# Relu²-attention and an MLP mixer on one core: another written order of all engines, with 56 stretches of small tiles

## The chip, the core and the metric

The kernel runs on one core of one Trainium2 chip. The metric is the device time of one execution in microseconds. A core has engines that run side by side, each with its own instruction stream: PE (TensorE, the matrix unit), DVE (VectorE), ACT (ScalarE), POOL (GpSimd, here only for issuing loads) and SP (SyncE, here for issuing transposes and stores). Matmuls write into PSUM, eight banks of 128 partitions by 512 fp32 columns; ACT and DVE read PSUM and write the on-chip memory SBUF, from which PE reads. An engine works through its stream in order. Where an instruction needs something another engine or a DMA has not finished, it waits, and all that is behind it on that engine waits too.

## The reference

Attention without softmax (relu, squared) over 8 batches, 12 heads, 448 positions and heads of 64, then a mixer over tokens and over channels:

```
scores = (q @ k.T) / sqrt(64)
attn   = maximum(scores, 0) ** 2 / 448
x      = (attn @ v)  -> (8, 448, 768)          # heads side by side
xt     = x.transpose(0, 2, 1)
h      = maximum(xt @ w_tok1, 0) @ w_tok2      # 448 -> 256 -> 448
u      = x + h.transpose(0, 2, 1)
out    = u + maximum(u @ w_ch1, 0) @ w_ch2     # 768 -> 1536 -> 768
```

Inputs and output are fp32; the kernel computes in bf16 with fp32 accumulation in PSUM.

## The kernel before

**Steps.** The attention is cut into 24 steps s of four heads, three to a batch. Each of its operations has a name with the step and a number behind it. The order in which all engines get their work is a string, `ORDER` (lines 73 to 242), with one word for each operation; `Order.run` (line 50) goes through the words and emits each operation's instructions, so the string is the order in every engine's stream at once. `:A` and `:D` send an operation to ACT or DVE; digits name the PSUM banks that it writes; a load's `:name` makes it wait until the SP operation of that name has been issued and done (line 971). Nothing moves the words at run time: what the planner of the string decided, the engines do. Dependencies, and the waits for a buffer's or a bank's former users, are semaphores.

The words, in the order in which a step goes through them:

- `ldk`, `ldq`, `ldv` (POOL, line 371): loads of half a step's k, q or v, 112 KB each, cast to bf16 on the way; four buffers for each. `ldf`, `cast` (ACT, DVE): step 0's q comes by SP as fp32 and is cast (lines 349 and 351 are the copies on ACT and on DVE that `cast`, `cp`, `xc`, `ik` and `iq` share). `wt1`, `wt2`, `wc1`, `wc2`: weights, `wc` in thirds of 768 KB.
- `T` (PE, line 472) and `cp`: steps 0 to 9 transpose k and q on PE, and `cp` copies them out of PSUM. From step 10 on `ik`, `iq` (a copy on ACT or DVE) and `xk`, `xq` (a transposing DMA issued by SP, line 497) do this. Three buffers (`NQ`) hold the transposed k and q, so `xk`, `xq` of step s wait for the last score of step s - 3.
- `S` (PE, line 515): scores, seven a step, four matmuls of 64 by 64 on quarters of the array, into two banks. `r` (two to an S): relu out of PSUM, on ACT (line 343) or DVE (345). `q` followed by two numbers: the square, on ACT (355) or DVE (357).
- `V` (PE, line 542): attention times v, again on quarters of the array, seven a step, accumulated in two banks. `xe`: eviction with the scale (ACT 552, DVE 554).
- `X` and `xc` (steps 0 to 5: PE transposes and copies them) or `xd` (from step 6: a transposing DMA of SP, line 566): x with the tokens on the partitions.
- `t1` (PE, 588), `rt` (relu on ACT), `t2` (PE, 597), `u` (DVE, 601): token mixing and the residual. `ub` (SP, line 610): u transposed back by DMA, for the last add.
- `C1`, `c1e` (line 623): channel mixing, first matrix, for batches 0 and 1. `M1`, with `tu`, `s1`, `d1`, `y1`, `w1` (function `fast1`, products at line 780): the same for batches 2 to 7 with seven products instead of eight; `tu` and `w1` are sums made ahead, `s1`, `d1`, `y1` take the products out of PSUM.
- `M2`, with `d2`, `h`, `w2` (function `fast2`, products at line 847; `d2` are DVE adds, lines 860 and 862) and, for tiles that have no partner, `C2`, `c2e`: channel mixing, second matrix, likewise, and the last add of u. `st` (SP, line 668): stores from four output buffers.
- `fill:bank*count` (line 967): matmuls on a buffer of zeros into a free bank, whose result nobody reads; a count of 4 is 512 columns, the rest units of 128.

**Stretches.** S, V and T work on small tiles (64 by 64 on a quartered array), all other products of PE on the full array. A stretch is a run of S, V and T with none of the others between them.

**What follows from the order.** SP's queue holds `xk`, `xq`, `xd`, `ub` and `st` in the order of the words; POOL's holds the loads. The operations of step s + 1 and later are written between those of step s, so that the evictions of one fill the time of PE's products of the other. The first 40 us have only attention and token mixing; the products of the channels begin when batch 0's u is there (`C1.0.3` is the first before).

The two places that the change touches in the code:

```python
    def run(self, fill):
        done = set()
        for word in ORDER.split():
            name, _, how = word.partition(':')
            if name == 'fill':
                bank, _, count = how.partition('*')
                fill(int(bank), int(count))
                continue
            o = self.ops[name]
```

```python
        for n in [512] * (count // 4) + [128] * (count % 4):
            nc.tensor.matmul(ps[:, :n], lhsT=warm[:, :128], rhs=warm[:, :n], start=True, stop=True)
```

Of the kernel before, what the change touches and what calls it, by code (L numbers as in the profile page):

```python
# [123 lines left out]
q9.6:D c1e1.11:A u6.1:D c1e1.8:A t2.7.0:1 ub1.4 c1e1.7:D V9.0:05 V9.1 u7.0:D S10.1:27 V9.2 V9.3 r10.1.1:A
h0.3.0:D S10.5:46 st2.64 V9.4 r10.1.0:A V9.5 r10.5.0:D V9.6 st0.0 S11.0:31 S10.4:72 xe9.1:A xe9.0:D M2.0.3.2:4
xk12 r10.4.1:A r10.5.1:D r11.0.1:A r11.0.0:D t2.7.1:5 r10.4.0:A d2.0.3.11a:D S10.0:02 xd9 S10.6:61 h0.3.1:D
S10.3:37 r10.0.0:A M2.0.3.5:4 u7.1:D r10.0.1:A ldk14.1:ub1.4 q11.0:A r10.6.0:D xq12 M2.0.3.1:0 ldv10.1:st2.64
iq13:D r10.3.1:A ik13:D r10.3.0:A M2.0.5.2:2 ub2.0 d2.0.3.11b:D r10.6.1:A h0.5.0:D S11.1:56 h0.3.2:D S10.2:73
t1.8.0:1 r10.2.1:A xk13 h0.3.3:D r11.1.0:A r10.2.0:D M2.0.3.6 rt8.0:A d2.0.5.11a:D ub2.2 r11.1.1:A q10.0:D
t2.8.0:3 q10.4:A d2.0.3.12a:D M2.0.5.1:5 d2.0.3.22a:D ub2.1 ldv11.1:xq12 u8.0:D S11.2:71 t2.8.1:2 ldq14.0  # L130
r11.2.0:A M2.0.3.3 r11.2.1:A u8.1:D ldv10.0:xq12 xq13 q10.2:A h0.5.1:D ldq14.1 t1.9.0:6 d2.0.5.11b:D q10.1:A
ldv11.0:xq12 tu2.2:D S11.3:37 ldk16.1:xk13 ik14:D S11.4:12 r11.3.1:A M2.0.3.7 h0.5.2:D ldv12.1:ub2.2 q11.2:A
r11.4.0:D ldq16.1:xk13 M2.0.5.6 r11.4.1:A d2.0.3.22b:D ldk16.0:ub2.1 r11.3.0:A h0.5.3:D M2.0.5.5:7 rt9.0:A
d2.0.5.12a:D q10.3:A ldq15.1 M2.0.3.4 d2.0.5.22a:D q11.4:A q11.1:D ldk15.1 M2.0.5.3 d2.0.3.12b:D q10.6:A
tu2.0:D ldv12.0:ub2.2 S12.0:12 d2.0.3.21:D q10.5:A V10.0:36 V10.1 w1.2.2:D V10.2 ldq15.0 S11.5:40 M2.0.5.7
r11.5.0:A r11.5.1:D ldq17.0:ub2.1 r12.0.0:A d2.0.5.12b:D ldk17.0 iq14:A M1.2.0.5:4 d2.0.5.22b:D ldk15.0
w1.2.1:D V10.3 r12.0.1:A V10.4 S11.6:01 q11.3:D V10.5 V10.6 xq14 S12.2:72 w1.2.0:D xe10.1:A M2.0.5.4 xe10.0:D
r12.2.0:A r11.6.1:D xk14 M1.2.0.1:6 s1.2.0.5:A tu2.1:D M1.2.2.1:3 r12.2.1:D s1.2.0.1:A M1.2.0.2:7 r11.6.0:D
# [865 lines left out]
```

## Time and profile before

| what | value |
| --- | --- |
| median of 3 runs | 346.09 us (344.8 to 348.53) |
| the profiled execution | span 345.2 us, one core |
| PE | first warm-up product (line 414) starts at 1.19 us, last product ends at 340.98 |
| DMA | 50.19 MB moved in 98939 packets, mean 145 GB/s |
| queue 1 (SP's and the transposes) | 45.8% of 16 engines' span |
| queue 0 (POOL's loads) | 45.2% of 16 engines' span |

The page gives, for each engine, its busy time and share of the span, then the same in 40 slices of 8.6 us, then the chain of work that ended last. PE's busy time counts the fills, and counts a matmul at half clock as busy for twice as long. The view by windows gives for a stretch of time the busy time of PE, PE's weight loads, DVE, ACT and POOL, each with the number of instructions, then the granted clock (1.00 is full), the DMA share and GB/s. A line of the timeline is: start, length, engine, line, operation, output and inputs, number of instructions, and in brackets the idle time before it and what ended that. A line of the chain is: start, length, engine, output or line, number.

### The profile page before, as it was taken

Reading aid. Unit: us, or ns where it says so; the run is one execution under the profiler, and the core shown is the slowest. Engines: PE = TensorE matmul, PEld = TensorE weight load, DVE = VectorE, ACT = ScalarE, POOL = GpSimd, SP = SyncE. Lnnn points to the kernel's source line nnn. Section 1 sums busy time; section 2 is a strip of 40 time slices with the busy share of each in tenths; the row PEclk is TensorE's granted clock in tenths of the full one; section 3 lists DMA queues with packets and bytes.
Section 4 is the critical chain, followed back from the end, with each engine's and each line's share of the span. In section 5 each row is a group of like instructions: output and inputs, shape, how many; then the busy total and the mean of one; then the engine's idle time right before and its main releaser. Section 6 shows DMA issues by size and latency. Waiting matters only on the chain.

```text
span 345.2 us, 9402 instructions
## 1 busy us (share of the span) xinstructions
PE 336.0 (97%) x3794; PEld 218.8 (63%) x3795; DVE 299.9 (87%) x578; ACT 243.4 (71%) x457; POOL 92.1 (27%) x157
## 2 busy tenths in 40 slices
PE   7899999999999999999999999999999999999995
...
GB/s 150 184 187 168 171 175 207 113 168 122 186 196 172 144 174 139 222 190 162 180 200 182 191 87 178 181 138 194 80 99 140 9 88 33 41 121 38 106 160 141
DMA packets 98939, 50.19 MB, mean 145 GB/s; under 512 B 71568, under 2 KB 95952, under 8 KB 98896
## 3 DMA queue, kind: packets, MB, share of 16 engines
q1 hardware_dynamic: 72880, 27.15, 45.8%
q0 software_dynamic: 25136, 21.47, 45.2%
...
q14 instruction: 14, 0.11, 0.1%
...
## 4 chain that ended last, share of the span: by engine, by line
PE 87%; DMA 6%; DVE 4%; SPq 1%; issue 0%; ACT 0%; DVEq 0%
PE m_ps L780 22%; PE m_ps L847 20%; PE sc_ps L515 10%; PE acc_ps L542 10%; PE m_ps L623 8%; PE t_ps L588 6%; PE h_ps L597 5%; PE m_ps L713 5%; DMA out_dram<-out_sb 2%; DMA u_sb<-uT 2%; DMA arena<-in_q_dram 1%; DVE arena L357 1%; PE kqT_ps L472 1%; DVE arena L345 1%; DVE arena L351 1%; PE x_ps L579 1%
## 5 line engine op out<-in xcount | busy, mean ns | idle before, releaser
L343 ACT ACTIVATE arena<-sc_ps 128x448 bf16<-128x448 f32 x238 | 117.3, 569 | 15.5 <-PE sc_ps L515 14.4
L345 DVE TENSOR_SCALAR arena<-sc_ps 128x448 bf16<-128x448 f32 x98 | 59.2, 618 | 4.2 <-PE sc_ps L515 2.6
L357 DVE TENSOR_TENSOR arena<-arena 128x896 bf16<-128x896 bf16 x105 | 61.9, 618 | 0.8 <-ACT arena L343 0.7
L355 ACT ACTIVATE arena<-arena 128x896 bf16<-128x896 bf16 x63 | 58.5, 960 | 0.2
L515 PE MATMUL sc_ps<-arena 64*64 64x448 bf16 x672 | 55.5, 370 | 1.1 <-DVE out_sb L860 0.4
L371 POOL DMA_DIRECT2D arena<-in_v_dram x48 | 29.5, 621 | 95.0 <-DMA out_dram<-out_sb 33.8
L542 PE MATMUL acc_ps<-arena 64*64 64x448 bf16 x672 | 46.2, 357 | 1.3 <-DVE arena L357 1.3
L780 PEld LDWEIGHTS <-wc 128*128 128x128 bf16 x432 | 40.8, 98 | 6.1 <-issue 3.2
L371 POOL DMA_DIRECT2D arena<-in_q_dram x46 | 28.3, 626 | 43.5 <-DMA u_sb<-uT 8.2
L371 POOL DMA_DIRECT2D arena<-in_k_dram x48 | 29.7, 626 | 26.9 <-DMA out_dram<-out_sb 16.1
L515 PEld LDWEIGHTS <-arena 64*64 64x64 bf16 x672 | 20.5, 107 | 21.5 <-issue 14.6
L780 PEld LDWEIGHTS <-ws 128*128 128x128 bf16 x324 | 30.5, 98 | 4.5 <-issue 2.5
L601 DVE TENSOR_TENSOR uT<-h_ps,xT 128x448 bf16<-128x448 f32 x48 | 29.2, 618 | 2.2 <-PE h_ps L597 2.1
L847 PE MATMUL m_ps<-wc,r 128*128 128x384 bf16 x162 | 30.3, 327 | 0.0
L847 PEld LDWEIGHTS <-r 128*128 128x128 bf16 x216 | 20.2, 98 | 15.9 <-issue 3.9
L623 PE MATMUL m_ps<-uT,wc 128*128 128x448 bf16 x144 | 30.1, 353 | 0.0
L542 PEld LDWEIGHTS <-arena 64*64 64x64 bf16 x672 | 20.5, 107 | 15.0 <-issue 6.0
L793 ACT ACTIVATE arena<-m_ps 128x448 f32<-128x448 f32 x18 | 9.4, 546 | 24.7 <-PE m_ps L780 7.6
L597 PE MATMUL h_ps<-wt,r_sb 128*128 128x448 bf16 x96 | 25.4, 353 | 0.0
L588 PE MATMUL t_ps<-x_sb,wt 128*128 128x256 bf16 (+1 forms) x216 | 25.4, 261 | 0.0
L780 PE MATMUL m_ps<-uT,wc 128*128 128x224 bf16 x216 | 25.0, 259 | 0.0
L847 PEld LDWEIGHTS <-sums 128*128 128x128 bf16 x180 | 17.2, 98 | 11.7 <-issue 1.1
...
## 6 DMA issues: line engine op xcount, KB each, us to landing
...
arena<-in_k_dram POOLq DMA_DIRECT2D x48, 112.0 KB, 4.4
arena<-in_v_dram POOLq DMA_DIRECT2D x48, 112.0 KB, 4.4
arena<-in_q_dram POOLq DMA_DIRECT2D x46, 112.0 KB, 4.5
wc<-in_moe_w_ch_dram POOLq DMA_DIRECT2D x6, 768.0 KB, 17.3
...
```

The source lines that it names most:

```text
L343: nc.scalar.activation(out, ps, AF.Relu)
L345: nc.vector.tensor_scalar(out=out, in0=ps, scalar1=0.0, scalar2=None, op0=ALU.max)
L355: nc.scalar.activation(x, x, AF.Square)
L357: nc.vector.tensor_tensor(out=x, in0=x, in1=x, op=ALU.mult)
L371: o.ins = nc.gpsimd.dma_start(out=raws[t][s % NR][64 * half:64 * (half + 1)], in_=src[b, h0:h0 + 2].rearrange('e (p c) d -> p e (c d)', c=KC))
L515: nc.tensor.matmul(o.ps[e][64 * half:64 * (half + 1), :S], lhsT=lhsT, rhs=rhs, start=True, stop=True, skip_group_check=True)
L542: nc.tensor.matmul(o.ps[half][64 * e:64 * (e + 1), :S], lhsT=r[rows, e, c * D:(c + 1) * D], rhs=sq[rows, e, :], start=c == 0, stop=c == KC ...
L588: nc.tensor.matmul(o.ps[:, j, :], lhsT=wt1[:, c, j * 128:(j + 1) * 128], rhs=x_sb[:, p0:p1, c, :], start=c == 0, stop=c == 3)
L597: nc.tensor.matmul(o.ps[:, :S], lhsT=r1[:, j, a * 128:(a + 1) * 128], rhs=wt2[:, j, :], start=j == 0, stop=j == JC - 1)
L623: nc.tensor.matmul(ps[:, :S], lhsT=wc1[:, g, e * 128:(e + 1) * 128], rhs=uT[:, g, off:off + S], start=g == 0, stop=g == CC - 1)
L780: nc.tensor.matmul(o.ps[:, j * HB:(j + 1) * HB], lhsT=lhs[:, g, (e + j) * 128:(e + j + 1) * 128], rhs=rhs[:, g], start=j == g == 0 and not ...
L847: nc.tensor.matmul(o.ps[:, :HN], lhsT=lhs[:, e], rhs=rhs[:, e], start=e == 0 and not on, stop=e == EC // 2 - 1, skip_group_check=True)
```

## The change

Only the string `ORDER` is replaced. Both strings hold the same operations; the words stand in another order, many operations change between ACT and DVE, banks are dealt out anew, the gates of the loads name other transposes and stores, and the fills differ. The string is one line longer, so the lines behind it have numbers larger by one.

Counted in the two strings:

| | before | after |
| --- | --- | --- |
| stretches of S, V and T | 68 | 56 |
| of these ahead of `t2.2.1` | 11 | 11 |
| fill words, and units of 128 columns | 4, 16 | 7, 68 |
| `r` on ACT, on DVE | 238, 98 | 216, 120 |
| `q` (square) on ACT, on DVE | 63, 105 | 82, 86 |
| `ik` on ACT | 1 | 7 |
| `c1e` on ACT | 18 | 15 |
| `xe` on ACT | 29 | 32 |
| `y1` on ACT | 11 | 13 |
| `rt` on ACT | 20 | 19 |

The start of both strings, and of the rest of the new one the rounds of `xq18`, `xq19` and `xq20`:

```diff
@@ -71,174 +71,175 @@
 ORDER = """
-ldf.0 ident ldf.1 ldk0.0 ldk0.1 ldk1.0 ldv2.0 cast0.0:D cast0.1:A ldq1.0 ldk1.1 cast1.0:D cast1.1:A ldq1.1
-fill:1*4 T0.0:0 ldv0.1 T0.1:1 cp0.0k:A cp0.0q:D ldv0.0 cp0.1k:D ldq2.0 cp0.1q:D ldk2.0 fill:4*7 S0.3:23
-S0.1:45 S0.6:67 r0.3.0:A r0.3.1:D ldq2.1 S0.5:01 r0.1.0:A r0.1.1:D S0.0:23 wt1.1 r0.6.0:A r0.6.1:D r0.0.0:A
-ldv1.1 q0.1:D r0.0.1:A ldk2.1 q0.3:D r0.5.0:A T1.0:45 r0.5.1:A q0.0:D S0.4:67 ldq3.0 S0.2:23 cp1.0:A cp1.1:D
-ldk3.0 q0.5:D V0.0:01 r0.2.0:A S1.2:54 V0.1 q0.6:D r0.2.1:A ldv1.0 r0.4.0:A r0.4.1:D S1.3:23 ldv2.1 r1.2.0:A
-q0.2:D r1.2.1:A wt1.0 q0.4:D r1.3.0:A V0.2 S1.1:67 ldv3.0 V0.3 q1.2:D r1.3.1:A V0.4 S1.4:54 r1.1.0:A ldk4.1
-r1.1.1:D S1.0:23 r1.4.0:A r1.4.1:D ldk3.1 S1.6:67 r1.0.0:A V0.5 V0.6 q1.1:D r1.0.1:A ldk4.0 xe0.1:D xe0.0:A
-ldq3.1 r1.6.0:A T2.0:54 q1.0:D r1.6.1:A q1.3:D X0.0:2 wt2 X0.1:3 cp2.0:A cp2.1:D S1.5:01 V1.0:67 ldq5.0 V1.1
-q1.4:D r1.5.0:A V1.2 S2.3:45 ldq4.1 V1.3 r1.5.1:A xc0.0:D V1.4 xc0.1:D r2.3.0:A ldk5.1 S2.0:02 q1.5:D r2.3.1:A
-S2.2:13 ldv4.0 q1.6:D r2.0.0:A fill:4*3 V1.5 S2.1:45 r2.0.1:A r2.2.0:D ldq6.1 r2.1.0:A r2.1.1:D S2.6:02 V1.6
-ldv3.1 r2.2.1:A t1.0.0:1 q2.0:D xe1.0:A ldq5.1 S2.4:45 xe1.1:D r2.6.0:A V2.0:36 r2.6.1:A q2.1:D X1.1:0 ldq4.0
-rt0.0:A q2.2:D r2.4.0:A fill:7*2 V2.1 S2.5:72 ldk6.0 q2.3:D r2.4.1:A V2.2 T3.0:14 r2.5.0:A xc1.1:D ldv5.0 V2.3
-q2.4:D r2.5.1:A t2.0.0:5 cp3.0:A ldk5.0 cp3.1:D t1.1.1:0 X1.0:7 u0.0:D wc1.0 rt1.1:A V2.4 S3.2:24 xc1.0:A
-q2.5:D t2.1.1:1 r3.2.0:A q2.6:D ldq6.0 S3.1:50 r3.2.1:A u1.1:D S3.4:72 ldk6.1 V2.5 r3.1.0:A V2.6 q3.2:D ub0.3
-t1.1.0:4 r3.1.1:A ldv4.1 xe2.1:D xe2.0:A S3.0:15 wc1.2 t1.0.1:0 r3.4.0:A r3.4.1:D X2.1:6 rt1.0:A q3.1:D X2.0:3
-r3.0.0:A wc2.0 S3.3:72 xc2.1:D rt0.1:A r3.0.1:A T4.0:41 xc2.0:D wc1.1 q3.4:D r3.3.0:A S3.6:60 t2.0.1:3
-r3.3.1:A cp4.0:D t1.2.1:5 wc2.2 r3.6.0:A u0.1:D S3.5:72 r3.6.1:A cp4.1:D t1.2.0:4 rt2.1:A t2.1.0:6 r3.5.0:A
-q3.0:D t2.2.1:3 rt2.0:A q3.3:D r3.5.1:A S4.1:05 S4.4:17 u1.0:D r4.1.0:A V3.0:42 V3.1 u2.1:D r4.1.1:A ub0.2
...
+fill:3*18 ident ldf.0 ldf.1 cast1.0:D ldk0.0 ldk0.1 cast0.0:D cast1.1:D cast0.1:A T0.0:0 cp0.0k:A T0.1:1
+cp0.0q:A fill:7*7 ldq1.0 ldv0.1 cp0.1k:D cp0.1q:D S0.3:24 r0.3.1:D r0.3.0:A S0.5:56 r0.5.0:D S0.2:30 r0.2.1:D
+r0.2.0:A ldq1.1 q0.3:D ldk2.1 ldk1.0 ldk1.1 S0.1:71 r0.1.1:A ldq2.0 S0.4:24 r0.4.0:A r0.4.1:D fill:3*3 S0.0:50
+r0.0.1:D r0.5.1:A S0.6:13 r0.6.0:A r0.1.0:A T1.0:26 cp1.0:A fill:4*24 cp1.1:D q0.2:D r0.0.0:D S1.1:10 q0.4:A
+q0.1:D r0.6.1:D r1.1.1:A S1.3:76 r1.3.1:A S1.0:24 r1.0.1:A r1.0.0:A r1.1.0:A q0.0:D S1.5:50 ldv0.0 V0.0:63
+r1.5.1:A q0.6:A wt2 ldk2.0 r1.3.0:D ldq2.1 wt1.1 S1.4:42 V0.1 q0.5:D T2.0:71 r1.5.0:D V0.2 V0.3 V0.4 r1.4.0:A
+S1.2:05 V0.5 V0.6 cp2.1:D q1.5:D r1.2.1:A xe0.0:A S1.6:14 r1.2.0:A ldv1.0 q1.1:D ldv2.0 ldv2.1 cp2.0:D S2.1:56
+r1.4.1:D xe0.1:A q1.3:A r2.1.0:D wt1.0 S2.2:07 ldq3.0 ldk3.0 r2.2.0:A r1.6.0:A r1.6.1:A X0.0:3 fill:5*8
+S2.0:25 r2.0.1:A q1.0:D q1.4:D r2.0.0:A r2.2.1:D X0.1:0 ldv1.1 V1.0:14 V1.1 r2.1.1:A S2.3:75 r2.3.1:A q1.2:D
+V1.2 V1.3 V1.4 r2.3.0:A xc0.1:D S2.6:20 xc0.0:D S2.4:63 r2.4.1:A r2.4.0:A q1.6:D ldq3.1 r2.6.0:D V1.5 V1.6
+xe1.1:D ldq4.1 xe1.0:A S2.5:57 r2.5.1:A q2.0:A q2.3:D q2.2:D ldk4.0 ldq5.1 ldk3.1 t1.0.1:2 fill:6*6 X1.0:3
+xc1.0:A t1.0.0:4 T3.0:61 cp3.0:A rt0.0:A fill:7*2 q2.1:D rt0.1:A ldq4.0 X1.1:7 t1.1.0:3 r2.5.0:D cp3.1:D
+S3.2:51 V2.0:64 r3.2.1:A q2.4:D rt1.0:A r2.6.1:D V2.1 V2.2 r3.2.0:A S3.0:20 r3.0.0:A ldk4.1 V2.3 V2.4 q2.5:D
+xc1.1:D T4.0:13 r3.0.1:A S3.1:75 V2.5 wc1.0 ldq5.0 q2.6:D r3.1.0:A cp4.1:D V2.6 xe2.1:A cp4.0:A ldk5.1 xe2.0:D
+r3.1.1:A ldv3.0 t2.0.1:2 u0.1:D t2.0.0:0 u0.0:D t1.1.1:3 rt1.1:A X2.0:7 xc2.0:D S3.4:64 r3.4.0:D S4.0:21
+r4.0.0:A r4.0.1:A S4.2:05 r4.2.1:D S4.3:73 r4.3.0:A r4.2.0:A r4.3.1:A r3.4.1:D X2.1:6 t2.1.0:2 t1.2.0:1 u1.0:D
+xc2.1:D S4.4:57 r4.4.0:D S3.6:40 ldv5.1 r4.4.1:A ldv4.0 ldk5.0 rt2.0:D ldv4.1 wc1.2 r3.6.1:A t2.1.1:2 u1.1:D
+t1.2.1:3 r3.6.0:A S4.1:67 r4.1.0:D T5.0:50 rt2.1:A S3.3:14 S3.5:23 r3.5.1:D r4.1.1:A q3.0:A ldv3.1 r3.5.0:A
+r3.3.1:A q3.4:A t2.2.1:7 q4.3:A u2.1:D q3.6:A t2.2.0:6 u2.0:D C1.0.1a:3 r3.3.0:D C1.0.2a:2 q3.1:D q3.3:D
+C1.0.3:7 c1e0.3:A C1.0.11:4 c1e0.11:A C1.0.1 c1e0.1:A q3.5:D cp5.1:D cp5.0:D q3.2:D C1.0.2 c1e0.2:D q4.0:D
...
+r17.3.0:A q16.1:D iq18:D r16.2.1:D M1.3.2.3 q17.0:A d1.3.2.12:D q16.3:D t1.14.0:7 M1.3.4.2:4 ub3.4 st13.64
+ik18:A rt14.0:A ldq20.1 M1.3.0.4 M1.3.2.7 q16.5:A d1.3.2.22:D M1.3.4.1:6 s1.3.4.1:A y1.3.0:D d1.3.4.11:D
...
+V16.5 V16.6 xk18 st12.0 r17.6.0:A r17.6.1:D xe16.1:A q17.6:A S17.5:64 h1.0.0:D S17.2:01 r17.2.1:D xq19 ub4.0
+t2.14.1:2 M2.1.2.2:5 r17.5.0:A r17.5.1:D M2.1.0.5:7 M2.1.0.2:1 u14.1:D r17.2.0:A d2.1.2.11a:D q17.5:D
+t2.14.0:4 q17.1:D h1.0.2:D xe16.0:A xq18 q17.4:A q17.2:A d2.1.0.11a:D u14.0:D S18.3:62 r18.3.1:A r18.3.0:A
...
+r19.2.0:A ldk21.0:st13.64 S19.3:60 r19.3.1:A ldk20.0:xd13 ldk21.1 ik20:D xd16 xk20 q19.0:D ub4.4 h1.2.0:D
...
+t2.15.1:0 q19.1:A q18.6:D q18.1:D ik21:A u15.1:D M2.1.2.7 d2.1.2.22b:D xk21 ldq23.0:xk21 iq20:A xq20 q18.4:A
...
+ik22:D xk22 tu4.0:D iq21:D r19.5.1:A S20.2:06 r20.2.1:A r20.2.0:A V18.5 V18.6 r19.6.0:A q20.2:A iq22:D xq22
```

More of the change, by code (lines that the diff above doesn't have):

```diff
@@ L124 @@
[L124 to L138, printed above, removed]
@@ L184 @@
-d2.1.0.12b:D rt17.0:A h1.2.3:D S18.5:06 d2.1.2.22a:D S18.6:25 S19.2:17 r18.5.0:D r18.6.1:A xk21 M2.1.2.7
-r19.2.0:A iq21:D q18.4:A r18.5.1:D t2.17.0:5 xq21 M2.1.2.3 d2.1.2.22b:D r18.6.0:A u17.0:D r19.2.1:A M2.1.2.4
-q18.5:A d2.1.2.12b:D ub4.4 iq22:D q18.6:A S19.4:01 q18.2:D S19.3:62 t1.16.0:7 st8.64 d2.1.2.21:D r19.3.0:A
-r19.4.1:D r19.4.0:A st9.64 S19.5:53 r19.3.1:A V18.0:46 V18.1 st7.64 rt16.0:A V18.2 r19.5.0:D S19.6:01 V18.3
-ik22:A ub5.0 r19.5.1:D V18.4 V18.5 S20.2:27 tu4.1:D V18.6 r20.2.1:A M1.4.0.5:5 q19.3:D r19.6.1:A xq22
@@ L189 @@
-M1.4.0.1:3 xe18.0:D xe18.1:A r20.2.0:D M1.4.0.2:7 s1.4.0.1:A t2.16.0:1 r19.6.0:A xd18 d1.4.0.11:D M1.4.0.6
-s1.4.0.5:A u16.0:D q19.5:A t2.16.1:4 ldv21.1:ub5.0 q19.2:D M1.4.2.1:6 xk22 ldk23.1:st9.64 s1.4.0.2:A u16.1:D
-M1.4.0.3 s1.4.2.1:A ldq23.0:xk21 M1.4.2.2:2 q19.4:A d1.4.0.12:D ub4.5 ldv20.1:xq22 M1.4.2.6 d1.4.2.11:D
-q19.6:A S20.0:07 S20.4:14 V19.0:52 r20.0.1:D st10.0 r20.0.0:A V19.1 V19.2 r20.4.1:D V19.3 r20.4.0:A V19.4
-V19.5 q20.0:D V19.6 S20.3:70 S20.1:14 xe19.0:A tu4.3:D M1.4.0.7 s1.4.2.2:A xe19.1:D r20.3.1:A M1.4.2.5:5
@@ new lines @@
+ldq19.0 ldq17.1:st4.0 q14.5:D q14.6:A rt12.0:D q14.3:A ldv14.0:ub2.3 d2.1.4.12b:D ldk17.1:st4.0 C2.1.6.0:6
+d2.1.4.21:D iq17:A r15.4.0:A u11.1:D tu3.2:D S15.0:07 r15.0.1:D r15.0.0:A c2e1.6.0:D V14.0:14 ik17:D V14.1
+V14.2 S15.3:52 V14.3 r15.3.1:D r15.3.0:A r15.4.1:A V14.4 V14.5 V14.6 xe14.1:D S15.5:07 r15.5.1:A xd13 S15.6:65
+r15.6.1:A ldv15.1:xd13 ub3.1 C2.1.6.1:3 xe14.0:A r15.5.0:A S15.2:27 r15.2.0:A xq16 ldv17.0:xq16 r15.6.0:D
+st6.64 xk16 S16.0:45 st12.64 st11.0 q15.6:A xk17 ldk18.1:xk17 t1.13.0:1 rt13.0:A xq17 S16.3:60 tu3.0:D q15.4:D
@@ new lines @@
+V17.0:05 V17.1 S18.0:31 r18.0.1:A xk19 r18.0.0:D ub4.3 V17.2 V17.3 V17.4 S18.1:24 V17.5 r18.1.1:A h1.0.1:D
+S19.0:63 r19.0.0:D r19.0.1:A V17.6 xe17.1:D xe17.0:A r18.1.0:A ldv18.1 M2.1.0.1:1 d2.1.0.11b:D ldq21.0:xq19
+ub4.1 ldk22.0:ub4.0 S19.1:43 r19.1.0:A r19.1.1:A ub3.5 d2.1.0.22a:D ldq22.1 ldk22.1 xd17 ub4.5 S18.4:60
+S18.2:52 r18.4.0:D r18.4.1:A r18.2.0:A h1.0.3:D M2.1.0.6 d2.1.0.12a:D ldv19.1:st13.0 S19.2:43 r19.2.1:A
+r19.2.0:A ldk21.0:st13.64 S19.3:60 r19.3.1:A ldk20.0:xd13 ldk21.1 ik20:D xd16 xk20 q19.0:D ub4.4 h1.2.0:D
```

257 lines of the change are left out of this document (132 added, 125 removed).

## The prediction

> **What bounds the kernel now.** I read the page from the top: the span, the busy shares, the slices.
>
> ```profile
> span 345.2 us, 9402 instructions
> PE 336.0 (97%) x3794; PEld 218.8 (63%) x3795; DVE 299.9 (87%) x578; ACT 243.4 (71%) x457; POOL 92.1 (27%) x157
> ...
> PE   7899999999999999999999999999999999999995
> ...
> PE m_ps L780 22%; PE m_ps L847 20%; PE sc_ps L515 10%; PE acc_ps L542 10%; PE m_ps L623 8%; PE t_ps L588 6%; PE h_ps L597 5%; PE m_ps L713 5%; DMA out_dram<-out_sb 2%; DMA u_sb<-uT 2%; DMA arena<-in_q_dram 1%; DVE arena L357 1%; PE kqT_ps L472 1%; DVE arena L345 1%; DVE arena L351 1%; PE x_ps L579 1%
> ```
>
> PE is the bound nearly everywhere, and the chain that ended last runs through it. Two things can still be won, though: a busy PE need not be a fast one, and the first slices are not full. So next the windows, to see who fills up early:
>
> ```profile
> 0.00:10.00 10.00, 7.90 (x90) 4.03 (x93) 3.63 (x13) 4.12 (x7) 9.26 (x20) 0.92 0.90 155
> 10.00:20.00 10.00, 8.43 (x193) 5.21 (x191) 9.23 (x18) 9.38 (x21) 9.75 (x18) 0.74 1.25 182
> 20.00:40.00 20.00, 19.70 (x413) 11.09 (x410) 20.00 (x41) 20.00 (x46) 12.31 (x19) 1.00 1.20 177
> 40.00:60.00 20.00, 20.00 (x236) 10.75 (x235) 19.25 (x37) 16.46 (x34) 2.55 (x4) 1.00 1.22 186
> ```
>
> From about 9 to 40 us DVE (third pair) and ACT (fourth) have no gap worth the name: the start is bound by them, and PE only seems busy. From 40 us on PE is the bound. Then the chain in order of time (start, length, what), for what one product costs:
>
> ```profile
> 49.49 0.69 PE sc_ps L515 x12
> ...
> 64.61 1.08 PE m_ps L847 x6
> ...
> 66.94 0.97 PE m_ps L847 x6
> ...
> 127.91 0.57 PE m_ps L780 x6
> ...
> 134.20 1.14 PE acc_ps L542 x24
> 135.53 0.68 PE m_ps L780 x6
> ```
>
> Six full-array matmuls of L780 take 0.57 us behind others of their kind, but 0.68 where V's matmuls on the quartered array stand ahead; L847 likewise, 0.97 and 1.08. So 0.11 goes at the way out of a stretch of small tiles. At the way in: 24 small matmuls take 1.14, four take 0.19, twelve should take 0.57, yet the twelve that end a stretch take 0.69, 0.12 more. A stretch costs about 0.23 us of PE.
>
> **The change part by part.** Counted in the two lists: every operation is in both; before has 68 stretches of small tiles (S, V, T), after 56; fill products come to 16 units of 128 columns before and 68 after. Engines change hands: ACT gets 19 more squares and 22 fewer relus of scores, and 7 instead of 1 of the ik copies.
>
> *1. The start, up to t2.2.1,* an operation that both lists have at the end of the start. Before, it waits on ACT:
>
> ```profile
> 35.27 0.20 PEld L597 LDWEIGHTS <-r_sb 128*128 128x128 bf16 x2 [0.18 <-ACT r_sb L343]
> ```
>
> It waits for rt2.1, which has 45 r, 5 rt, 4 cp, 3 xe, 2 cast and 1 xc at or ahead of it on ACT. After, t2.2.1 needs the bank that r4.1.1 frees, with 42 r, 5 rt, 5 cp, 4 xe, 1 cast, 1 xc and 4 squares. ACT's prices, by the timeline:
>
> ```profile
> 6.75 0.55 ACT L349 ACTIVATE arena<-kqT_ps 128x448 bf16<-128x448 bf16 x1
> ...
> 18.47 0.54 ACT L552 ACTIVATE xT<-acc_ps 128x448 bf16<-128x448 f32 x1
> 18.91 0.97 ACT L343 ACTIVATE arena<-sc_ps 128x448 bf16<-128x448 f32 x2
> ...
> 20.56 3.63 ACT L343 ACTIVATE arena<-sc_ps 128x448 bf16<-128x448 f32 x8
> ...
> 69.97 1.78 ACT L355 ACTIVATE arena<-arena 128x896 bf16<-128x896 bf16 x2
> ```
>
> Eight relus in 3.63, so one more costs 0.44; a square 0.82 (1.78 for two, 0.96 for one); the xe at 18.47 lets the next begin 0.44 later. Three r fewer (-1.3), four squares (+3.3), one half copy (+0.55), one xe (+0.44), one cast fewer (-0.6): ACT has 2.4 us more ahead of it. And it starts later:
>
> ```profile
> 4.12 0.39 DVE L351 CAST arena<-arena 64x448 bf16<-64x448 f32 x1 [2.42 <-DMA arena<-in_q_dram]
> ...
> 5.80 1.38 PE L472 MATMUL kqT_ps<-ident,arena 64*64 64x64 bf16 x56 [0.38 <-DMA arena<-in_k_dram]
> 6.15 0.49 DVE L351 CAST arena<-arena 64x448 bf16<-64x448 f32 x1 [1.64 <-DMA arena<-in_q_dram]
> ...
> 8.86 3.35 ACT L343 ACTIVATE arena<-sc_ps 128x448 bf16<-128x448 f32 x7 [1.57 <-PE sc_ps L515]
> ```
>
> DVE now has cast1.0 first, whose data lands at 6.15, and cast0.0 behind it, done near 7.0: T0.0 starts some 1.2 us after its 5.80, and the longer fill ahead of it costs nothing, since it covers that wait. T0.1 follows at once where it used to wait, so the first relu is late by between 0 and 1.2; I take 0.7. So t2.2.1 starts at 35.4 + 2.4 + 0.7 = 38.5, 3.1 later. But five S (0.19 each) and one T (about 0.5) now stand ahead of it that stood behind, 1.45 us of work done. The start loses 1.6 us, between 0.9 and 2.9 (no late start; late by the full 1.2 and 0.8 of gaps on ACT at cp1.0, which waits for T1.0 behind all seven S of the first step).
>
> *2. The 52 more fill units.* A C1 product moves 448 columns in 0.19, so they take 2.8 us of PE. All fills stand ahead of t2.2.1, where ACT, not PE, is late; they are inside the 38.5. Cost nothing; if that cover is gone, up to 2.8.
>
> *3. The stretches.* Ahead of t2.2.1 stand 11 in both lists. Behind it 57 before, 45 after: 12 x 0.23 = -2.8 us, on the path, as PE is full there. Not below -3.0 (0.25 each), nor above -1.3 (if only the way out counts).
>
> *4. Waits of before that go.* PE waits in two places behind 40 us, by the timeline and, in the second fence, the chain:
>
> ```profile
> 126.45 0.38 PE L515 MATMUL sc_ps<-arena 64*64 64x448 bf16 x3 [0.36 <-DVE out_sb L860]
> ...
> 212.33 1.14 PE L847 MATMUL m_ps<-wc,sums 128*128 128x384 bf16 x6
> 214.14 1.14 PE L847 MATMUL m_ps<-ws,r 128*128 128x384 bf16 x6 [0.67 <-DVE out_sb L862]
> ```
>
> ```profile
> 118.34 6.89 DMA u_sb<-uT
> ...
> 203.16 8.20 DMA out_dram<-out_sb
> ```
>
> The second product comes 0.84 after it could (1.81 against 0.97), the first some 0.75. Behind both is a late landing: ub2 holds up tu2 on DVE, a store holds up the out tile's next user. After, by the lists and the prices above, PE has 15 us of work between the add that triggers the last ub2 and tu2.0, against 9.5, and 36 between the add that triggers the store and its waiter, d2.1.2.22a, against 11.3. I take both as gone: -1.6, between -1.6 and 0.
>
> *5. New waits.* Loads, transposes and stores all move in SP's and POOL's order, and q18, q19, q20 and k10, k16, k17, k23 stand closer to their users. The landing times (median, last number) by the page:
>
> ```profile
> arena<-in_k_dram POOLq DMA_DIRECT2D x48, 112.0 KB, 4.4
> ...
> u_sb<-uT SPq DMA_TRANSPOSE x36, 4.8
> ...
> arena<-arena SPq DMA_TRANSPOSE x28, 4.9
> x_sb<-xT SPq DMA_TRANSPOSE x18, 3.9
> ```
>
> and what SP pays for issuing one, by the timeline and by the rows of L610:
>
> ```profile
> 112.23 1.44 SPq L497 DMA_TRANSPOSE arena<-arena  x1
> ...
> L610 SPq DMA_TRANSPOSE u_sb<-uT x36: 1178/1279/2620, 30.3 to 277.2; - x36
> ```
>
> The closest: xq18 stands on SP behind xq19 and ub4.0, and xq19 may not start before S16.6 has freed its buffer. From there PE has 9.9 us of work until S18.3 (5 S, 7 V, 4 M1, 3 M2, 3 t2, 1 t1). Two issues of 1.44 ahead of it and 4.9 to land make 7.8: in time. xq20 waits on ACT for three relus and two 0.82s (3.0), on SP for xk21 (1.4), then 4.9: 9.3 against 10.1. In time, barely. ub3.5 is seventh on SP behind S16.6: six issues of 1.3 and 4.8 make 12.6, against 13.6 of PE work until d2.1.0.22a can start. xd needs one evict and 3.9, with 9.0 or more (7.5 before). Early, wc1.2 is issued behind the load that V1.6 frees, about 28 us by the list, and C1.0.11 needs it near 42: 14 us, where the two wc1 issued before took 9.2 and 14.9.
>
> ```profile
> wc<-in_moe_w_ch_dram POOLq DMA_DIRECT2D x1, 768.0 KB, 9.2
> ...
> wc<-in_moe_w_ch_dram POOLq DMA_DIRECT2D x1, 768.0 KB, 14.9
> ```
>
> The first stands nearer, since wc1.0 goes out eight loads earlier now. ACT and DVE round trips (PE's end to evict to bank free) are as tight as before in most places and in some 20 a little tighter. I take 0.7 for all of it, between 0 and 7.
>
> *The tail* keeps its order: last product, last add, last store. Nothing.
>
> Sum against this execution: 345.2 + 1.6 - 2.8 - 1.6 + 0.7 = 343.1. The median of the runs, 346.09, is 0.9 above this span, so 344.0.
>
> **The rivals.**
>
> *Faster by over 1%.* No late start (+0.9), 0.25 per stretch (-3.0), no new wait: 345.2 + 0.9 - 3.0 - 1.6 = 341.5, or 342.4. For it: the start's only new order on DVE is one cast. Against: two queues that must come just in time.
>
> *No change.* The fills are not covered, because ACT is not what is late: +2.8, so 346.8. For it: PE at half clock (0.74 in 10 to 20 us) doubles each fill. Against: ACT's 20.00 of 20. "TensorE: Matmul & The Clock Gate" of the Trainium skill, under "What's actually happening", says that the array runs at half rate unless the last window of some 3.4 us was busy; the 0.74 agrees. By that page the fills buy a full clock, and by it too a start with more idle PE could fall back to half: one such window past 20 us would cost up to 1.7, so 345.7, inside this rival. That stretches save nothing since ACT or DVE set the pace all through the attention would come to the same 346.8; against it PE's 20.00 of 20 from 40 us on.
>
> *Slower.* The transposes land late. At 6.9 us, as at 118.34, with the two issues ahead of it at the longest 2.6 instead of 1.44, xq18 needs 12.1 against 9.9, and S18.3 stands 2.2 us with all PE behind it; xq20 is 1 late; ub3.5 is 1 to 2 late; five more S have 10.5 to 11.6 from trigger to use (15.2 was the least before). If each costs 1 to 2, it is about 8 in place of 0.7: 350.4, or 351.3. It decides from a landing of about 7 us on. For it: DMA shares over 1 up to 240 us in the windows. Against: half of the landings are under 4.9.
>
> **How the numbers follow.** The forecast (342.7 to 345.4) has 0.45, faster 0.18, no change 0.22, slower 0.15. Predicted 344.0. The range goes from 341.8 to 349.0: it leaves out the lower half of the faster case and most of the slower one. A measurement of this kernel can tell about 1% from no change, so: faster than 342.6, the whole faster case and a little of the forecast's edge, 0.20; slower than 349.6, 0.14; same 0.66.
>
> **What would show it.** T0.0 near 7.0, t2.2.1 near 38.5 and right behind an ACT evict; PE's fills inside gaps. Fewer 0.68 and 1.08 rows in the chain, 56 stretches. No wait of PE on a DVE add that a landing holds up. It is wrong if PE starts t2.2.1 after 40 us, if a fill stands directly ahead of a late S, if S18.3, S20.2 or C1.0.11 starts behind a DMA, or if ACT shows gaps before 35 us.

## The result, and the profile after

The changed kernel takes 362.96 us in the median of four runs (358.57 to 365.86), the kernel before 345.8 us. The ratio is 1.0395 with an interval of 1.0319 to 1.047. Ratios here and below leave out runs more than 1.5% above the fastest of the same kernel (here 358.57 and 360.75 stay), so they can be lower than the ratio of the medians. The profiled execution has a span of 359.0 us against 345.2: 13.8 us more. The forecast was 344.0 with a range up to 349.0, so it was wrong, and on the wrong side.

The page of the changed kernel, span and busy times, and the chain's shares:

```profile
span 359.0 us, 9469 instructions
PE 339.7 (95%) x3811; PEld 223.5 (62%) x3811; DVE 301.1 (84%) x575; ACT 254.4 (71%) x460; POOL 91.9 (26%) x157
...
PE m_ps L848 22%; PE m_ps L781 17%; PE sc_ps L516 9%; PE acc_ps L543 8%; DMA x_sb<-xT 7%; PE m_ps L624 6%; PE t_ps L589 6%; PE h_ps L598 5%; PE m_ps L714 4%; DMA u_sb<-uT 2%; DMA arena<-in_q_dram 1%; DVE arena L346 1%; ACT arena L344 1%; PE kqT_ps L473 1%; PE x_ps L580 1%
```

PE is still the bound by its share, but the chain now holds `DMA x_sb<-xT` with 7%, which was not in it before: the transposing DMA `xd`. The windows of the changed kernel (PE, PE's loads, DVE, ACT, POOL, then granted clock, DMA share, GB/s):

```profile
0.00:10.00 10.00, 8.74 (x91) 4.02 (x92) 3.14 (x11) 3.23 (x5) 8.98 (x20) 1.00 0.87 150
10.00:20.00 10.00, 7.99 (x191) 4.41 (x188) 9.97 (x20) 9.84 (x21) 8.68 (x16) 1.00 1.24 182
20.00:40.00 20.00, 19.23 (x396) 12.64 (x397) 19.23 (x38) 19.73 (x43) 12.44 (x20) 1.00 1.20 188
40.00:60.00 20.00, 20.00 (x295) 10.78 (x294) 19.16 (x37) 17.76 (x30) 3.70 (x6) 1.00 1.21 198
...
100.00:140.00 40.00, 37.69 (x372) 21.92 (x372) 33.99 (x66) 32.45 (x57) 10.09 (x17) 0.96 1.03 146
...
180.00:220.00 40.00, 36.74 (x381) 24.40 (x378) 33.55 (x63) 33.33 (x62) 13.09 (x23) 0.96 1.17 168
```

Up to 60 us nothing is lost against the forecast: the granted clock is 1.00 in each window and PE has no gap from 40 to 60. Behind that PE has gaps, and the clock falls to 0.96 in places. What PE waited for, in the view of waits (in total, times, longest):

```profile
PE t_ps L589 <- DMA x_sb<-xT: 6.2, 4, 3.0
PE sc_ps L516 <- DVE arena L346: 3.2, 1, 3.2
...
PE sc_ps L516 <- ACT xT L553: 1.0, 1, 1.0
```

The first row is `t1` waiting for `xd`, four times. The second is S19.3; its bank is freed by a relu that stands on DVE behind d2.1.0.22a, and DVE itself waited there 3.6 us for `ub3.5`. The third is S10.4. The view names an evict, but that one's banks are not S10.4's; what S10.4 reads comes by xk10, which landed at 106.81, 13.1 us after its issue, and S10.4 started at 106.85. The chain shows transfers behind these waits, with start and length:

```profile
92.23 9.02 DMA x_sb<-xT
...
146.49 8.53 DMA x_sb<-xT
...
204.59 7.89 DMA u_sb<-uT
...
236.93 8.48 DMA x_sb<-xT
```

They are xd7, xd11, ub3.5 and xd18, each 7.9 to 9.0 us, where the medians before were 3.9 for `xd` and 4.8 for `ub`. The other wait of `t1` is for xd10, which took 6.9.

The 13.8 us, summed from the timelines of the two executions, each PE operation from its start to the start of the next against what it takes among its own kind:

| part | before | after | difference |
| --- | --- | --- | --- |
| `t2.2.1` starts | 35.37 | 38.28 | +2.9 |
| PE's own work behind it | 284.7 | 283.1 | -1.5 |
| ways into and out of stretches behind it | 114 ways, 12.2 | 90 ways, 8.8 | -3.4 |
| other gaps under 0.16 | 5.4 | 6.0 | +0.6 |
| waits of PE, and work at half clock | 2.2 | 17.4 | +15.2 |
| last product to the end of the span | 4.22 | 4.24 | 0 |

The last row but one is the whole of the miss. (The last product's own 1.1 us stands in no row, and is the same in both.) Where a way ends and a wait begins is a matter of counting: with at most 0.11 for a way, the ways come to 11.3 and 9.0, and the row of waits to 2.0 and 15.9.

What had changed around the late transposes is POOL. Its timeline in the changed kernel:

```profile
91.01 0.59 POOL L372 DMA_DIRECT2D arena<-in_q_dram  x1 [12.24 <-DVE arena L352]
91.59 1.20 POOL L372 DMA_DIRECT2D arena<-in_k_dram  x2
92.76 0.64 POOL L372 DMA_DIRECT2D arena<-in_v_dram  x1
...
95.93 0.61 POOL L372 DMA_DIRECT2D arena<-in_q_dram  x1
97.98 0.59 POOL L372 DMA_DIRECT2D arena<-in_k_dram  x1 [1.44 <-DMA arena<-in_k_dram]
```

Before, the loads of the same stretch went out like this:

```profile
89.00 1.20 POOL L371 DMA_DIRECT2D arena<-in_v_dram  x2 [8.36 <-DMA x_sb<-xT]
92.38 0.60 POOL L371 DMA_DIRECT2D arena<-in_v_dram  x1 [2.18 <-DMA out_dram<-out_sb]
92.96 0.61 POOL L371 DMA_DIRECT2D arena<-in_k_dram  x1
95.81 0.60 POOL L371 DMA_DIRECT2D arena<-in_q_dram  x1 [2.24 <-PE sc_ps L515]
99.39 1.30 POOL L371 DMA_DIRECT2D arena<-in_k_dram  x2 [2.98 <-DMA arena<-arena]
```

The load at 91.01 in the changed kernel is ldq14.0. It waited 12.24 us for the copy `iq10` to free its buffer, and the eight loads behind it, five of them ready before it, then went out one after the other, most of them 0.58 us apart, and a ninth at 97.98. The changed kernel has four such runs of nine loads. In the same window stand xq10, xd7 and xk10. In the list before, ldq14.0 stands twelve loads further back. One sentence ahead of the prediction is to be corrected here: the gates of the loads are the same in both strings, all 57 of them; it is only the order of the loads that differs.

### The profile page after: what moved, and what is told of

The parts are those of the page before. It is cut to its first block, busy times and chain, and to the rows that moved or that the text cites. A ratio compares the mean times of both kernels' runs of the same rounds, so it can differ in the third digit from the quotient of the medians.

```text
span 359.0 us, 9469 instructions
## 1 busy us (share of the span) xinstructions
PE 339.7 (95%) x3811; PEld 223.5 (62%) x3811; DVE 301.1 (84%) x575; ACT 254.4 (71%) x460; POOL 91.9 (26%) x157
## 4 chain that ended last, share of the span: by engine, by line
PE 80%; DMA 11%; DVE 4%; ACT 3%; issue 1%; SPq 1%; DVEq 0%
PE m_ps L848 22%; PE m_ps L781 17%; PE sc_ps L516 9%; PE acc_ps L543 8%; DMA x_sb<-xT 7%; PE m_ps L624 6%; PE t_ps L589 6%; PE h_ps L598 5%; PE m_ps L714 4%; DMA u_sb<-uT 2%; DMA arena<-in_q_dram 1%; DVE arena L346 1%; ACT arena L344 1%; PE kqT_ps L473 1%; PE x_ps L580 1%
## 5 line engine op out<-in xcount | busy, mean ns | idle before, releaser
L344 ACT ACTIVATE arena<-sc_ps 128x448 bf16<-128x448 f32 x216 | 107.7, 562 | 23.5 <-PE sc_ps L516 22.7
L356 ACT ACTIVATE arena<-arena 128x896 bf16<-128x896 bf16 x82 | 76.7, 972 | 0.2
L346 DVE TENSOR_SCALAR arena<-sc_ps 128x448 bf16<-128x448 f32 x120 | 71.4, 618 | 5.9 <-PE sc_ps L516 5.3
L516 PE MATMUL sc_ps<-arena 64*64 64x448 bf16 x672 | 54.0, 360 | 5.4 <-DVE arena L346 3.2
L358 DVE TENSOR_TENSOR arena<-arena 128x896 bf16<-128x896 bf16 x86 | 51.8, 618 | 0.8 <-ACT arena L344 0.6
L543 PE MATMUL acc_ps<-arena 64*64 64x448 bf16 x672 | 44.3, 359 | 0.9 <-ACT arena L344 0.9
L516 PEld LDWEIGHTS <-arena 64*64 64x64 bf16 x672 | 21.2, 105 | 26.7 <-issue 16.6
L848 PEld LDWEIGHTS <-r 128*128 128x128 bf16 x216 | 20.7, 99 | 15.9 <-issue 3.3
L543 PEld LDWEIGHTS <-arena 64*64 64x64 bf16 x672 | 21.5, 109 | 12.3 <-issue 2.5
L589 PEld LDWEIGHTS <-wt 128*128 128x128 bf16 x216 | 18.9, 98 | 11.8 <-DMA x_sb<-xT 6.3
L797 DVE CUSTOM_DVE_ANT_0 r<-r,m_ps 128x448 bf16<-128x448 f32 x32 | 19.5, 618 | 6.8 <-PE m_ps L781 4.0
L848 PEld LDWEIGHTS <-sums 128*128 128x128 bf16 x180 | 17.4, 99 | 12.3 <-issue 2.3
```

Source lines behind the costliest of these rows:

```text
L344: nc.scalar.activation(out, ps, AF.Relu)
L346: nc.vector.tensor_scalar(out=out, in0=ps, scalar1=0.0, scalar2=None, op0=ALU.max)
L356: nc.scalar.activation(x, x, AF.Square)
L358: nc.vector.tensor_tensor(out=x, in0=x, in1=x, op=ALU.mult)
L516: nc.tensor.matmul(o.ps[e][64 * half:64 * (half + 1), :S], lhsT=lhsT, rhs=rhs, start=True, stop=True, skip_group_check=True)
L543: nc.tensor.matmul(o.ps[half][64 * e:64 * (e + 1), :S], lhsT=r[rows, e, c * D:(c + 1) * D], rhs=sq[rows, e, :], start=c == 0, stop=c == KC ...
```

## The experiments

**Theory L** came from this view: loads in a burst make the transposes late. Its rivals: SP's own order (S), and PE's order leaving its users too near (D); S and D together are called Q further on.

**Whole queues exchanged.** Four kernels take the order of one queue from one list and put it, nearly unchanged, into the other. The first one's loads, from the 77th on:

```diff
-ldq14.0 ldk12.0 ldk13.0:st1.0 ldv9.0:xd6 ldq14.1 ldv9.1:st2.0 ldq15.0 ldk15.1 ldq13.0:st1.0
+ldk12.0 ldv9.0:xd6 ldv9.1:st2.0 ldk12.1:st1.64 ldq13.1:xd7 ldk13.1:xq11 ldk14.0:xk11 ldk13.0:st1.0
...
```

> The changed list, but from the 77th load on the loads stand on POOL in the order of the list before (gates are the same in both); all other engines as in the changed list. Theory L (load order): in the changed list a load whose buffer is late stands ahead of eight to ten that are ready, they then go out 0.58 us apart, and transposes that share the DMA engines with them take 7 to 13 us instead of 4 to 5. Then PE's waits and half-clock stretches behind t2.2.1 fall from 17.4 us to 3 to 6 and the span from 359.0 to 345 to 349. Theory S (SP order): SP's own order makes the transposes late; then nothing much changes, 355 to 362. Theory D (distance): the users stand too close by PE's order; 355 to 362 as well.

Measured: 367.77 us, ratio 1.0544 (1.0451 to 1.0636). No theory had that. Its chain says why:

```profile
136.36 7.56 DMA x_sb<-xT
...
181.80 7.37 DMA arena<-in_v_dram
...
224.77 9.96 DMA arena<-arena
```

The waits for xd7, xk10, xd11, xd14, ub3.5 and xd18 are gone (they take 3.2 to 5.3 us here), as L says, and of the `xd` only xd10 (7.56) still holds up `t1`. A new one is late: xq20, in the last row, takes 9.96 with ten loads around it, and S20.2 waits 2.4 us for it. And now a load is late itself: ldv15.0, in the middle row, goes out at 181.80 and V15.0 starts the moment it has landed, after a wait of 7.7 us. The old order fits the old list's events, and on the new one its gates hold loads back until their users need them. The run speaks for L at these places and says nothing on the total.

> The list before, but from the 77th load on the loads stand on POOL in the order of the changed list. Theory L: the loads come in bursts and at least some transposes land late in a kernel that had no such waits: 350 to 358. Theories S and D: within 1% of before, 343 to 349.

Measured: 390.31 us, 1.1219 (1.1147 to 1.1291). Slower as L says, but not by L's means: its longest waits (12.5, 7.4, 7.5 and 8.9 us) are again for loads that come too late: ldk12.1, ldk17.1, ldk20.0 and ldk21.1. Inconclusive.

In the next two, SP's queue is exchanged:

```diff
-xd6 ub1.4 st1.64 xq10 xd7 xk10 st0.64 xk11 xq11 ub2.2 ub1.3 xd8
+xk10 xd6 st1.64 xq10 st2.0 xd7 st0.64 xq11 xk11 ub1.0 ub1.2 st1.0 ub1.5 ub1.1 xd8
...
```

> The changed list, but SP's transposes and stores from the ninth on in the order of the list before (nine of them moved ahead where another engine needs them); loads as in the changed list. Theory S: 345 to 350. Theories L and D: 354 or more, since the bursts are still there; it may be slower than the changed kernel, where SP now waits for work that this list does late.

> The list before, but SP's transposes and stores from the ninth on in the order of the changed list. Theory S: 350 to 358. Theories L and D: within 1% of before, 343 to 349, or a few us slower where SP waits for a store that this list does late.

Measured: 408.15 us (1.1758, 1.1658 to 1.1857) and 403.26 us (1.1596, 1.1511 to 1.1681). Both are far out. In the first, SP waits in order for work that this list does late: xd6 lands after 3.2 us but goes out 7.3 us after it was ready. What holds up the second isn't shown. They rule out that before's SP order as a whole would have saved the changed list, and show nothing more.

**Only the loads dealt out again.** The next edits change nothing but the loads of the changed list, sorted by when they are needed. Of the 76 from ldq14.0's place on, 60 are gated, on 52 SP operations:

```diff
-ldq14.0 ldk12.0 ldk13.0:st1.0 ldv9.0:xd6 ldq14.1 ldv9.1:st2.0 ldq15.0 ldk15.1 ldq13.0:st1.0
+ldv9.0 ldv9.1 ldk12.0 ldk12.1 ldv10.1:st1.0 ldq13.0 ldq13.1 ldk13.0:ub1.4 ldk13.1:st1.64 ldk14.1:xq10
...
```

> The changed list with its loads from the 77th on dealt out again: sorted by when they are needed, each behind an SP operation of its own, so that they go out about 1.8 us apart instead of 0.58 apart in bursts of eight to ten; every other engine's order is the changed list's. Theory L (bursts of loads make the transposes late): no transpose of 7 us or more holds up PE, PE's waits and half-clock stretches behind t2.2.1 fall from 17.4 us to 2 to 4, the span from 359.0 to 343 to 346, and the ratio to before is 0.99 to 1.005. Theory Q (SP's own order makes them late, or the distances that PE's order leaves): at least half of the waits stay, 351 to 360.

Measured: 347.24 us, ratio 1.0026 (1.0004 to 1.0047), profiled span 346.6. The same products, SP order, ACT and DVE order as the changed kernel, and 12.4 us of its 13.8 are gone. The span is a little above the 343 to 346 expected, the ratio within its range. In the trace the loads aren't evenly spaced, but the longest run of them has six, where the changed kernel has nine. The page and the view of waits:

```profile
span 346.6 us, 9492 instructions
```

```profile
PE t_ps L589 <- DMA x_sb<-xT: 1.8, 1, 1.8
...
PE sc_ps L516 <- DVE arena L352: 0.9, 1, 0.9
PE acc_ps L543 <- ACT arena L344: 0.9, 1, 0.9
```

Of four waits for `xd` one is left (xd7, 6.84 us), and PE's waits and half-clock work behind `t2.2.1` come to 4.6 us against 17.4, a little over the 2 to 4 expected (3.3 against 15.9 by the other count). The 3.2 us at S19.3 are gone without ub3.5 having been moved on SP. Theory L's forecast holds nearly; Q's 351 to 360 does not. That SP's order or the distances alone make the transposes late is ruled out, since neither was changed.

> The list before with its loads from the 77th on dealt out in the same way, 1.8 us apart. Theory L: the two waits of before for late landings (1.6 us) go or stay, nothing new comes: 343 to 346 in the median. Theory Q: the same as before within 1 us. It is here mainly as the partner of the paced changed list: with loads paced in both, the difference is that of the other engines' orders, by the sum of the prediction (start +1.6, stretches -2.8) about -1 us.

Measured: 350.6 us, 1.012 (1.0072 to 1.0168): a miss. Dealt out by the same rule, the loads of the list before do 1.2% worse than by its own order. Its profiled execution (span 352.6) is the longest of six; xq16 (6.64 us) and xd17 (7.97) take long there, and whether they do in the others isn't shown. So pacing as such is no gain. The comparison that the expectation had planned, paced against paced, gives 347.24 against 350.6, 3.4 us where about 1 was expected; as what b_paced's shorter runs wait for isn't shown, it says little on the other engines' orders.

For one burst alone:

```diff
-ldq14.0 ldk12.0 ldk13.0:st1.0 ldv9.0:xd6 ldq14.1 ldv9.1:st2.0 ldq15.0 ldk15.1 ldq13.0:st1.0 ldk14.1:ub1.4
+ldk12.0 ldv9.0:xd6 ldv9.1:xd6 ldk13.0:xq10 ldq13.0:xd7 ldq14.0:xd7 ldq14.1:xk10 ldk14.1:xk10 ldq15.0:xk11 ldk15.1:xq11
```

> The changed list with only its first burst taken apart (ten loads, from ldq14.0 to ldk14.1: the four that are needed first stay in front, six wait one by one for xd7, xk10, xk11 and xq11). Theory L: xd7 and xk10 land in 4 to 6 us, the waits at t1.7.0 and S10.4 and the half clock between them (5.5 us) go, the others stay: span 351 to 355. Theory Q: xd7 and xk10 are still late, 357 to 361.

Measured: 350.27 to 361.15 us over four runs, 357.21 in the median, ratio 1.0154 (1.0094 to 1.0214); the profiled span is 348.5. In the profile xd7 and xk10 take 5.4 and 5.2 us instead of 9.0 and 13.1 and hold up nothing, as expected. The rest was not foreseen: the waits for xd10, xd11, xd14 and xd18 are gone in this execution too, though their loads were not touched. The last three still take 7.2 to 7.3 us, but land 1.0 to 1.5 us ahead of their users; ub3.5 still costs 2.6 us. This is the shortest of the four runs. What the others wait for, up to 11 us longer, isn't shown, and on the total the run is unclear.

**The gates left out, before.** The same from the other side: nothing is moved, only the 51 gates are taken off the loads of the list before.

```diff
-ldv9.0:xd6 ldv8.1 ldv9.1:st2.0 ldk12.1:st1.64 ldq13.1:xd7 ldk13.1:xq11 ldk14.0:xk11
+ldv9.0 ldv8.1 ldv9.1 ldk12.1 ldq13.1 ldk13.1 ldk14.0
...
```

> The list before with the 51 gates of its loads from the 77th on left out: the same order on every engine, but a load goes out as soon as its buffer is free and the loads ahead of it are out. Theory L: loads come earlier and in longer bursts, some of them on top of transposes: 348 to 358, with transposes of 8 us and more and waits of PE behind them. If order alone matters and bursts do no harm: 343 to 347.

Measured: 369.45 us, 1.065 (1.0599 to 1.0702), more than expected. Its waits and its chain:

```profile
PE t_ps L588 <- DMA x_sb<-xT: 12.4, 7, 4.3
```

```profile
85.41 10.95 DMA x_sb<-xT
...
178.27 14.83 DMA arena<-arena
...
193.10 12.75 DMA x_sb<-xT
```

No order was touched, no distance shortened. A kernel whose PE never waited for `xd` does so seven times once loads go out whenever they can. Together with a_paced this shows that the times at which loads go out make the transposes late.

How the landing goes with the loads, worked out from the issues and landings of all transposes behind 80 us (loads counted that are under way when the transpose is issued or go out in the 4 us behind; median and longest time to landing):

| loads | before | after | b_no_gates |
| --- | --- | --- | --- |
| 0 or 1 | 27: 3.0, 5.2 | 28: 3.0, 5.3 | 45: 3.2, 4.8 |
| 2 or 3 | 29: 4.6, 6.9 | 24: 4.1, 7.1 | 5: 4.9, 5.4 |
| 4 or 5 | 23: 5.4, 7.3 | 17: 5.3, 8.5 | 14: 6.3, 9.4 |
| 6 or 7 | 8: 5.8, 8.6 | 8: 6.6, 8.4 | 6: 7.3, 9.4 |
| 8 or more | 1: 4.9, 4.9 | 9: 8.9, 13.1 | 18: 10.3, 14.9 |

In all three kernels the landing takes longer from row to row (but for the one transpose in the last row before), and within a row they differ by at most 1.5 us in the median up to seven loads; the kernels differ most in how many transposes stand in the last row. The paced list has none there. The list before has bursts as well (eleven loads from 167 us on), but hardly a transpose under them. The Trainium skill, "DMA: Bandwidth & Descriptors", under "Issuing engines are not separate DMA queues", says that transfers started by different engines run on the same 16 DMA engines and interleave; the table agrees.

A rival is that SP's own transfers crowd each other. With at most one load, in these three kernels and the paced one, the median landing goes from 2.95 us with no other transfer of SP under way to 3.27 with three or more, so by themselves they do little. The count of loads isn't all, though. Of the late transposes xd7, xk10, xd14 and ub3.5 had eight to ten loads, but xd10 had three, xd11 and xd18 four each, and they took 6.9 to 8.5. What makes these three so long isn't isolated; that they depend on the loads too is shown by the paced list, which moves nothing else and ends their waits.

**The fills.** In the paced list:

```diff
-fill:3*18 ... fill:7*7 ... fill:3*3 ... fill:4*24 ... fill:5*8 ... fill:6*6 ... fill:7*2
+fill:3*4 ... fill:7*7 ... fill:3*3 ... fill:7*2
```

> The paced changed list with 16 units of fill products as the list before has, instead of 68. By the prediction the 52 units cost nothing, since ACT is what is late at the start: within 0.7 us of the paced list with all fills, and t2.2.1 within 0.5 us. If they are on PE's path: 1 to 3 us faster. If they buy the full clock (1.00 in the first 20 us, 0.92 and 0.74 before): the granted clock falls to 0.7 to 0.9 there, and t2.2.1 comes 0.5 to 3 us later.

Measured: 348.99 us against 347.24 for the paced list with all fills. `t2.2.1` starts at 40.48 instead of 38.60. Windows of the kernel with few fills:

```profile
0.00:10.00 10.00, 7.78 (x90) 3.87 (x90) 3.82 (x12) 3.72 (x6) 8.69 (x20) 0.90 0.88 150
10.00:20.00 10.00, 7.36 (x185) 4.11 (x179) 9.29 (x19) 9.22 (x19) 7.44 (x13) 0.76 1.14 163
```

The same of the paced list with all fills:

```profile
0.00:10.00 10.00, 7.61 (x95) 3.92 (x95) 3.26 (x12) 3.56 (x6) 8.99 (x20) 1.00 0.90 152
10.00:20.00 10.00, 7.99 (x197) 4.45 (x195) 9.97 (x19) 9.84 (x21) 8.83 (x16) 1.00 1.23 181
```

The third outcome came: the fills buy the clock, and 2.8 us of products in gaps gain 1.9. This agrees with the rule that the prediction cites from the Trainium skill, "TensorE: Matmul & The Clock Gate".

**Mending the rest.** Three more versions of the paced list look for one that beats both kernels.

```diff
-st1.64 xq10 xd7 xk10
+st1.64 xd7 xq10 xk10
...
```

> The paced changed list with two more edits: xd7 stands on SP ahead of xq10 instead of behind it, and no load is dealt into the 3.6 us around the issue of fourteen transposes that were nearest to being late. Theory L: the 1.96 us that PE still waits for xd7 go, the rest of its waits stays near that of the list before (2.7 us): 344 to 346 in the median, ratio 0.992 to 1.000. If landings are late whatever the loads do: 347 or more.

Measured: 348.44 us, 1.0055 (1.0029 to 1.0081): a miss. xd7 goes out at 89.72 instead of 93.53 and lands at 99.38 instead of 100.37, after 9.66 us, with four loads by the count of the table. Issued earlier, it only took longer among the loads and stores that were under way.

```diff
-fill:3*18 ... cast1.0:D ... cast0.0:D
+fill:3*9 ... cast0.0:D ... cast1.0:D
```

> The same with the start mended: on DVE cast0.0 stands ahead of cast1.0 as in the list before, and the first fill is 9 units instead of 18. By the prediction the new order of the casts makes the first relu 0 to 1.2 us late (0.7 taken): T0.0 near 6.2 instead of 7.0, t2.2.1 0 to 1.2 us earlier, the median 0 to 1.2 us less than without. If the shorter fill costs the clock (under 1.00 in the first 20 us), t2.2.1 is later instead, by 0.5 to 2 us.

Measured: 346.37 us, 1.0006 (0.9979 to 1.0033). The median is 2.1 less, by the ratios 1.7, but not as expected: `t2.2.1` starts at 38.58 (38.19 without the edit), the first relu at 8.87 (9.15), and the clock is 1.00. The cast's place does not set the end of the start; what made the time lower is open.

```diff
-xd6 ub1.4 st1.64 xd7 xq10 xk10 st0.64 xk11 xq11 ub2.2
+xd6 xd7 xq10 xk10 st0.64 xk11 xq11 ub1.4 st1.64 ub2.2
-ldv10.1:st1.0 ldv10.0:ub1.0 ldq13.0 ldq13.1:xd6
+ldv10.1:st1.0 ldq13.0:xd7 ldq13.1:xd7
...
```

> The last version (paced, start mended) with the two late landings that are left taken out: around xd7 two other SP operations (ub1.4, st1.64) and three loads now come behind it, around xd18 three SP operations and five loads. Theory L: xd7 lands in 4 to 6 us instead of 8.0, xd18 in 3 to 5 instead of 6.7, the waits at t1.7.0 and t1.18.0 go (about 1 us together), and the median is 344.5 to 346, ratio 0.995 to 1.000. Otherwise, if other waits take their place: 346.4 or more.

Measured: 346.5 us, 0.9997 (0.9971 to 1.0023). xd7 takes 5.2 us and xd18 3.3, neither holds up PE; xd9 (6.8) and ub3.5 (6.1) come late instead, and PE's waits stay at 4.1 us. No version beats the kernel before; the best are equal to it.

## Why the prediction was wrong

*The start* was right: 38.28 for `t2.2.1` against 38.5 forecast, and +2.9 - 1.5 = +1.4 against +1.6. Its inner split is not borne out. In the changed kernel's profile T0.0 starts at 7.07 because the fill of 18 units, which takes 2.1 us, ends then. In the paced list, with the same start, the fill takes 1.1, T0.0 starts at 6.22 and its products wait 0.7 us for the cast on DVE, as the prediction had it; but putting the cast back brought the first relu only 0.28 us forward, and `t2.2.1` not at all.

*The fills* cost nothing, as said, but not for the reason given alone. The rival that they would cost 2.8 was wrong; its second half, that a start with more idle PE falls back to half clock and loses up to 1.7, is what taking them away showed (1.9).

*The stretches* were right in kind: 24 ways fewer. By the table they saved 3.4, more than the 3.0 given as the most, and the other small gaps took 0.6, together -2.8; with at most 0.11 a way they saved 2.3. That the sum is the forecast to a tenth is partly luck.

*The two old waits* went: nothing waits for ub2 at tu2.0 or for st13.0 at d2.1.2.22a.

*The new waits* were the step that failed: 0.7 was taken, and PE's waits and half-clock work came to 17.4. The sentence that failed is "xd needs one evict and 3.9, with 9.0 or more". The distances were long enough: from the last evict to `t1` the late ones had 9.3 to 14.2 us. The 3.9 was not: it is a median of the kernel before, and it holds for before's order of the loads only. Nor was it all that stood between evict and `t1`: SP issued the five late ones (xd7, xd10, xd11, xd14, xd18) 2.3 to 5.6 us after the evict, and issuing xd10 alone took 4.9 where the prediction took 1.44. In the paced list the same five still wait 1.7 to 4.0 on SP, land in 3.1 to 6.8, and only xd7 holds up PE: the landing is the larger part. The prediction compared each load with its own user (wc1.2 came in time, as it said) and never asked what a load does to a transfer of another queue. xq18 and xq20, named as the closest, came in time (2.1 and 2.5 us to spare); ub3.5, the seventh on SP, was late as the rival had it.

*The rival "slower"* had the mechanism, late transposes from a landing of about 7 us on, and of its places ub3.5; S18.3 and S20.2, which it named too, did not wait for theirs. It was priced at 351.3 and given 0.15, and the range stopped short of it. Its price was too low by half: it counted no `xd`, and no half clock behind the waits. One row each, in the changed kernel's timeline, for that half clock:

```profile
101.30 1.05 PE L589 MATMUL t_ps<-x_sb,wt 128*128 128x256 bf16 x8 [2.99 <-DMA x_sb<-xT]
...
103.01 1.34 PE L543 MATMUL acc_ps<-arena 64*64 64x448 bf16 x12
```

Behind the wait, twelve matmuls of V take 1.34 us, where 24 took 1.14 in the prediction's row. The granted clock is 0.50 from 102.75 to 106.10, and again from 215.40 to 218.70 behind S19.3 (the 0.96 in the windows above); between them it is 1.00, also behind the waits of 1.1 to 1.3 us for xd10 and xd11. A wait of 3 us thus cost 1 to 2 us more.
